# A windowed attention and channel mix on one core: unit 0's q and k loaded in halves of four heads, with all orders and choices found anew

## The chip, the core and the metric

One core of a Trainium2 chip runs the whole program. PE is the matrix engine, ACT, DVE and POOL are the scalar, vector and general engines, and SP issues the DMA transfers. The metric is the device time of one execution in microseconds; lower is better.

## The reference

Attention over 4 batches of 8 heads, 768 positions and head size 64, with a window of 128 positions and 4 sink positions that every query sees; its output is the input `x` of a channel mix with a shift by one position.

```python
scores = scale * np.matmul(q, k.transpose(0, 1, 3, 2))
keep = is_sink | ((rel >= 0) & (rel < window))        # rel = query position - key position
scores = np.where(keep, scores, -1e9)
a = softmax(scores);  attn = np.matmul(a, v)          # (4, 8, 768, 64)
x = attn.transpose(0, 2, 1, 3).reshape(4, 768, 512)
xk = mu_k * x + (1 - mu_k) * x_prev                   # x_prev: x, one position later
xr = mu_r * x + (1 - mu_r) * x_prev
k = np.maximum(xk @ w_k, 0.0)                         # 512 x 1024
v = k * k @ w_v                                       # 1024 x 512
out = 1 / (1 + np.exp(-(xr @ w_r))) * v
```

## The kernel before

The work is cut into 12 units `u` of 256 positions, three for each batch (T = 0, 1, 2). For each unit the kernel does four things.

`load` issues the transfers of q, k and v from SP's queue into fp32 buffers (`qs`, `ks`, `vs`, three each). For the early units a buffer holds eight heads as 1 KB pieces (four positions of one head), and two transfers of 64 partitions each bring one tensor: one for each value of `w`, and each brings pieces of all eight heads.

`prepare` casts a half (four heads) at a time to bf16 (`kb`, `qb`, on ACT, DVE or POOL), transposes it on PE into a bank, and copies the bank to `kt` or `qt` (ACT or DVE). Units from 4 (k) and 8 (q) on are transposed by DMA instead. `vb` is v in bf16, also cast by one of the three engines. A half's cast waits for both transfers of its tensor.

`attend` makes scores for two heads at a time into one of two tiles `sc`, in pairs (chunks 0 and 2, then 1 and 3; a chunk is two heads). ACT writes the exponentials (`e`), DVE multiplies them by a mask (`e<-e,mask`), or, in units 0 and 1, PE has added the mask's bias to `sc` beforehand. The sink positions have scores and exponentials of their own (`es`). PE multiplies by `vb`, DVE divides (`rec`, `x`).

`mix` transposes `x` to `xt` and forms `td`, `xk` and `xr` on DVE. `ffn` makes the products: eight blocks with w_k (`keys`, 32 matmuls of 256 columns), ReLU and square (`rl`, `kk`, on ACT or DVE), the gate with w_r (`gate`, and `th` on ACT), and the values with w_v (`product`), which DVE multiplies by the gate and SP stores. The weights come as fp32 (`w`) and are cast on chip in quarters (`wk_sb`, `wv_h`) or halves (`wr_sb`).

No scheduler orders this when the program is built. Each step is an operation with a number, in the order in which the code makes it. Three tables, found beforehand by a search with planned durations and written out as numbers, decide the rest: `ORDER` is the order in which operations are emitted, and so the order of each engine's queue and of SP's; a negative number there is a fill, a matmul on `warm` with no use. `CHOICE` gives an operation to another engine than its usual one. `SLOTS` says which buffer of a pool each tile takes. An engine takes its instructions strictly in that order, and waits at each for the semaphores that it needs.

Of the kernel before, what the change touches and what calls it, by code (L numbers as in the profile page):

```python
# [8 lines left out]
FP32 = mybir.dt.float32  # L9
# [9 lines left out]
    92: "ACT", 93: "ACT", 94: "ACT", 95: "ACT", 97: "ACT", 100: "ACT", 102: "DVE", 105: "DVE",  # L19
    110: "DVE", 111: "DVE", 114: "ACT", 115: "DVE", 139: "POOL", 142: "POOL", 145: "POOL", 148:  # L20
    "DVE", 150: "DVE", 151: "ACT", 152: "ACT", 154: "DVE", 161: "DVE", 191: "DVE", 193: "DVE",
    194: "DVE", 197: "DVE", 199: "DVE", 200: "DVE", 203: "DVE", 204: "DVE", 213: "DVE", 230:
    "ACT", 234: "ACT", 273: "DVE", 276: "DVE", 279: "DVE", 282: "DVE", 285: "ACT", 286: "ACT",
    298: "DVE", 306: "DVE", 315: "ACT", 354: "DVE", 364: "ACT", 365: "DVE", 367: "DVE", 383:
    "ACT", 387: "ACT", 436: "DVE", 439: "DVE", 444: "DVE", 445: "DVE", 467: "ACT", 475: "ACT",
    514: "DVE", 516: "DVE", 521: "DVE", 524: "ACT", 525: "ACT", 546: "ACT", 550: "ACT", 554:
    "ACT", 558: "ACT", 595: "DVE", 598: "DVE", 603: "ACT", 604: "ACT", 606: "DVE", 634: "ACT",
    681: "DVE", 682: "DVE", 691: "DVE", 700: "ACT", 704: "ACT", 708: "ACT", 755: "DVE", 759:
    "DVE", 760: "ACT", 772: "DVE", 781: "ACT", 785: "ACT", 789: "ACT", 834: "DVE", 836: "DVE",
    837: "DVE", 853: "ACT", 856: "DVE", 857: "ACT", 860: "DVE", 861: "ACT", 904: "DVE", 906:  # L30
    "DVE", 910: "DVE", 912: "DVE", 913: "DVE", 929: "ACT", 933: "ACT", 940: "DVE", 941: "ACT",
    994: "DVE", 995: "ACT", 999: "ACT", 1003: "ACT", 1007: "ACT", 1022: "DVE", 1026: "DVE",
    1034: "DVE", 1035: "ACT",
# [20 lines left out]

VS = ()
# [130 lines left out]
def kernel(  # L186
# [14 lines left out]
    nc = tc.nc  # L201
# [14 lines left out]
    P = Plan()  # L216
# [28 lines left out]
    buf = P.buf  # L245
# [829 lines left out]
```

## Time and profile before

| | |
|---|---|
| timed runs, median of 3 (lowest, highest) | 165.98 us (165.54 to 166.24) |
| profiled execution: span from first to last instruction | 164.3 us; the page gives no other time of it |
| PE busy, DVE, ACT, POOL | 158.4, 145.4, 131.2, 13.5 us |
| DMA | 34.6 MB, 79042 packets, 86.3% of 16 engines' span in SP's queue |
| fill matmuls (L1018) | 30 |

Busy times overlap. PE's matmuls are pipelined and their ends are modelled, so the spacing of their starts says more than their durations. A line of the timeline gives the start, the busy time, the engine, the line of the kernel, the operation, what is written and read, how many instructions are merged, and in brackets how long the engine sat idle before and what released it. SPq is SP's DMA queue; its time is that of issuing, not of moving bytes.

### The profile page before, as it was taken

To read this page: it belongs to the slowest core of one execution; us is meant where nothing else is said; L and a number is where in the kernel's file an instruction comes from. 1 tells how busy PE (TensorE), PEld (TensorE's weight loads), DVE (VectorE), ACT (ScalarE), POOL (GpSimd) and SP (SyncE) were. 2 spreads that over 40 slices of the span, in tenths; PEclk is the share of its full clock that TensorE was granted. 3 is DMA by queue.
4 is the path that set the end of the run, shared out by engine and by line. 5 is a ranking of instruction groups with operands and counts; after the bars stand their busy time and mean duration, and the time that the engine had idled before them with its cause. 6 is when DMAs were issued, how large, how long until landed. Compare 5 with 4: busy or idle time off the path is not lost.

```text
span 164.3 us, 4195 instructions
## 1 busy us (share of the span) xinstructions
PE 158.4 (96%) x1603; PEld 102.6 (62%) x1603; DVE 145.4 (89%) x381; ACT 131.2 (80%) x218; POOL 13.5 (8%) x38
## 2 busy tenths in 40 slices
PE   6999889999999999999999999999999999999992
PEld 2455568866467587577566775856575765664851
DVE  5259999999999999989999999999999999789752
ACT  3277999999999999999999999997668759163240
POOL 6409300010000000060000000000000000000000
PEclk9999999999999999999999999999999999999999
DMA  4999999999969896999999887986996955077743
GB/s 120 247 305 311 348 335 355 301 354 210 228 154 270 135 240 148 234 198 167 224 216 157 188 156 163 235 146 150 199 123 136 362 149 200 0 90 297 262 185 128
DMA packets 79042, 34.60 MB, mean 211 GB/s; under 512 B 67112, under 2 KB 73520, under 8 KB 79024
## 3 DMA queue, kind: packets, MB, share of 16 engines
q1 hardware_dynamic: 79008, 34.35, 86.3%
q8 instruction: 12, 0.20, 0.6%
q14 instruction: 6, 0.05, 0.1%
q10 hardware_dynamic: 16, 0.00, 0.0%
HBM read 24.12 MB, written 6.29 MB: 185 GB/s over the span
## 4 chain that ended last, share of the span: by engine, by line
PE 79%; ACT 8%; SPq 4%; DMA 3%; issue 2%; DVE 1%; POOL 1%; DVEq 0%; ACTq 0%; POOLq 0%
PE bank L997 23%; PE bank L939 23%; PE bank L979 12%; PE bank L808 6%; PE sc L721 6%; SPq L337 3%; DMA qs<-in_q_dram 3%; PE bank L576 2%; ACT e L775 2%; PE bank L849 2%; ACT rl L949 1%; PE bank L763 1%; ACT qt L589 1%; PE bank L909 1%; PE bank L1018 1%
## 5 line engine op out<-in xcount | busy, mean ns | idle before, releaser
L775 ACT ACTIVATE e<-sc 128x1024 bf16<-128x1024 f32 (+1 forms) x48 | 46.1, 994 | 1.8 <-PE sc L721 1.7
L939 PE MATMUL bank<-xk,wk_sb 128*128 128x256 bf16 x384 | 47.1, 273 | 0.0
L997 PE MATMUL bank<-wv_h,kk 128*128 128x512 bf16 x184 | 43.1, 379 | 0.1
L939 PEld LDWEIGHTS <-wk_sb 128*128 128x128 bf16 x384 | 36.4, 98 | 7.4 <-issue 0.4
L949 ACT ACTIVATE rl<-bank 128x512 bf16<-128x512 f32 x40 | 24.2, 625 | 8.6 <-PE bank L939 7.1
L997 PEld LDWEIGHTS <-kk 128*128 128x128 bf16 x184 | 17.1, 98 | 17.8 <-issue 0.4
L789 DVE TENSOR_TENSOR e<-e,mask 128x1024 bf16<-128x1024 bf16 (+1 forms) x40 | 25.4, 642 | 0.7 <-ACT e L775 0.5
L979 PE MATMUL bank<-wr_sb,xr 128*128 128x512 bf16 x96 | 23.7, 379 | 0.0
L888 DVE SCALAR_TENSOR_TENSOR xk<-td,mu_all,xt 128x256 bf16<-128x256 bf16 x48 | 22.4, 483 | 0.3
L888 DVE SCALAR_TENSOR_TENSOR xr<-td,mu_all,xt 128x256 bf16<-128x256 bf16 x48 | 22.1, 475 | 0.2
L967 ACT ACTIVATE kk<-rl 128x512 bf16<-128x512 bf16 x29 | 18.3, 664 | 4.2 <-DVE rl L953 4.0
L985 ACT ACTIVATE th<-bank 128x512 f32<-128x512 f32 x24 | 15.1, 646 | 5.7 <-PE bank L979 5.7
L825 DVE TENSOR_TENSOR x<-bank,rec 128x256 bf16<-128x256 f32 x48 | 19.2, 416 | 0.4
L808 PE MATMUL bank<-vb,e 128*128 128x65 bf16 x352 | 16.6, 194 | 0.0
L1006 DVE SCALAR_TENSOR_TENSOR w<-th,bank 128x512 f32<-128x512 f32 x19 | 13.0, 682 | 3.6 <-issue 1.8
L808 PEld LDWEIGHTS <-e 128*128 128x128 bf16 x352 | 13.6, 97 | 3.5
L979 PEld LDWEIGHTS <-xr 128*128 128x128 bf16 x96 | 8.8, 98 | 8.6 <-issue 0.2
L721 PE MATMUL sc<-qt,kt 64*128 64x128 bf16 (+1 forms) x256 | 13.9, 238 | 0.0
L721 PEld LDWEIGHTS <-kt 64*128 64x128 bf16 x256 | 8.9, 94 | 5.7 <-issue 3.1
L1018 PE MATMUL bank<-warm 128*128 128x512 bf16 x30 | 10.6, 484 | 1.1 <-DVE warm L1038 1.1
L877 DVE TENSOR_TENSOR td<-xt 128x512 bf16<-128x512 bf16 x24 | 10.3, 428 | 0.7 <-ACT xt L858 0.5
L589 ACT COPY qt<-bank 128x512 bf16<-128x512 bf16 x15 | 9.4, 643 | 1.0 <-PE bank L576 1.0
(74 smaller groups left out, 161.7 us busy)
## 6 DMA issues: line engine op xcount, KB each, us to landing
ks<-in_k_dram SPq DMA_DIRECT2D x24, 256.0 KB, 4.7
qs<-in_q_dram SPq DMA_DIRECT2D x24, 256.0 KB, 4.4
vs<-in_v_dram SPq DMA_DIRECT2D x24, 256.0 KB, 4.4
out_dram<-w SPq DMA_DIRECT2D x19, 256.0 KB, 2.7
w<-in_moe_w_k_dram SPq DMA_DIRECT2D x2, 1024.0 KB, 10.4
w<-in_moe_w_v_dram SPq DMA_DIRECT2D x2, 1024.0 KB, 9.3
w<-in_moe_w_r_dram SPq DMA_DIRECT2D x1, 1024.0 KB, 9.7
out_dram<-ob SPq DMA_DIRECT2D x4, 256.0 KB, 2.6
```

Source lines behind the costliest of these rows:

```text
L721: nc.tensor.matmul(out=sc[:, a, o0:o1], lhsT=lhs[rows], rhs=rhs[rows], start=u not in BIAS, stop=True, skip_group_check=u in BIAS)
L775: nc.scalar.activation(out=buf[ek][:, :, lo:], in_=buf[sck][:, :, lo:], func=AF.Exp, scale=scale)
L789: nc.vector.tensor_tensor(out=at, in0=at, in1=m, op=ALU.mult)
L808: nc.tensor.matmul(out=o[:, g, a, :], lhsT=e[:, a, e0:e0 + 128], rhs=rhs, start=(T == 0 and i == 0), stop=(i == len(blocks) - 1), skip_gro ...
L825: P.op("DVE", dve(256), lambda ok=ok, rk=rk, c=c: nc.vector.tensor_tensor(out=buf["x", u][:, :, 128 * c:128 * c + 128].rearrange("p g (a d ...
L888: nc.vector.scalar_tensor_tensor(out=buf[key][:, c, :], in0=buf[tk][:, i, :], scalar=mu[w][:, c:c + 1], in1=xt[:, c, t0 - 1:t0 + 255], op0 ...
L939: nc.tensor.matmul(out=ps[:, i, :], lhsT=wk_sb[:, c, 128 * f:128 * f + 128], rhs=xk[:, c, :], start=(c == 0), stop=(c == NC - 1), skip_gro ...
L949: nc.scalar.activation(out=buf[rk], in_=buf[psk].rearrange("p (i t) -> p i t", i=2), func=AF.Relu)
L967: nc.scalar.activation(out=buf["kk", u][:, 2 * f2:2 * f2 + 2, :], in_=buf[rk], func=AF.Square)
L979: nc.tensor.matmul(out=buf[psk], lhsT=buf["xr", u][:, c, 128 * g:128 * g + 128], rhs=wr_sb[:, c, :], start=(c == 0), stop=(c == NC - 1))
L985: P.op("ACT", act(512), lambda psk=psk, tk=tk: nc.scalar.activation(out=buf[tk], in_=buf[psk], func=AF.Tanh, scale=0.5), rank + 4 + g, tak ...
L997: nc.tensor.matmul(out=buf[psk], rhs=wv_h[:, f, :], lhsT=buf["kk", u][:, f, 128 * g:128 * g + 128], start=(f == 0), stop=(f == NF - 1))
```

## The change

Unit 0's q and k come head-wise. Each of the four transfers becomes two, of four heads each: 64 partitions with two pieces of 1 KB instead of four. Both transfers of the first half of q are issued first, then the two of k's first half. A half's cast waits only for its own two transfers. Further, 20 memsets of one column follow the mask on POOL. The steps and what they compute are the same otherwise. All three tables are new.

```diff
+BY_HALF = (0,)
...
 CHOICE = {
-    92: "ACT", 93: "ACT", 94: "ACT", 95: "ACT", 97: "ACT", 100: "ACT", 102: "DVE", 105: "DVE",
+    92: "DVE", 93: "ACT", 94: "ACT", 95: "DVE", 96: "DVE", 97: "DVE", 98: "DVE", 99: "ACT", 100:
...
 ORDER = (
-    80, 81, 78, 82, 87, 83, 84, 77, -1, -2, -3, -4, -1, -2, 90, 0, 1, 79, 102, 108, -2, -3, -4,
+    83, 81, 80, 78, 82, 2, 77, 0, 1, 3, 4, 5, 8, 9, 79, 105, -1, -2, -3, -4, -1, -2, -3, -4, 106,
...
+            if u in BY_HALF:
+                rows = src[b, :, 256 * T:256 * T + 256, :].rearrange(
+                    "(w l) (p j) d -> w p l (j d)", w=2, j=4)
+
+                def by_half(key=key, rows=rows, half=0):
+                    for w in range(2):
+                        nc.sync.dma_start(
+                            out=buf[key][w::2, 4 * half:4 * half + 4, :, :].rearrange(
+                                "p (l x) j d -> p l (x j d)", x=2),
+                            in_=rows[w][:, 2 * half:2 * half + 2])
+
+                for half in range(2):
+                    P.op("SP", 650.0, lambda f=by_half, half=half: f(half=half), rank,
+                         service=800.0, descs=256,
+                         take=[] if half else [(name + "s", key)], hold=[key] if half else [],
+                         writes=[(name, u, half, w) for w in range(2)])
+                continue
...
+    spare = tile1([128, 20], FP32, "spare")
+
+    def short(engine, lo, hi):
+        for i in range(lo, hi):
+            engine.memset(spare[:, i:i + 1], 0.0)
...
     def make_mask():
         window_mask(mask.rearrange("p k q -> p (k q)"), ones, 0.0)
+        short(nc.gpsimd, 0, 20)
```

In the listings below `x2` counts equal rows, and the number behind a name is that of the buffer. First SP's queue at the start of the program: ks_67 and qs_70 take unit 0, ks_68 and qs_71 unit 1, ks_69 and qs_72 unit 2. Before:

```order
L337 DMA ks_67<-in_k_dram 64x4x256 x2
L337 DMA qs_70<-in_q_dram 64x4x256 x2
L307 DMA vs_73<-in_v_dram 128x8x64 x2
L337 DMA ks_68<-in_k_dram 64x4x256
L337 DMA qs_71<-in_q_dram 64x4x256 x2
L337 DMA ks_68<-in_k_dram 64x4x256
L307 DMA vs_74<-in_v_dram 128x8x64
```

And in the change:

```order
L355 DMA qs_70<-in_q_dram 64x2x256 x2
L355 DMA ks_67<-in_k_dram 64x2x256 x4
L355 DMA qs_70<-in_q_dram 64x2x256 x2
L322 DMA vs_73<-in_v_dram 128x8x64 x2
L370 DMA qs_71<-in_q_dram 64x4x256 x2
L370 DMA ks_68<-in_k_dram 64x4x256 x2
```

Eight transfers stand ahead of v's instead of four, and unit 1's k is whole before anything of unit 1's v.

Next ACT's queue from unit 1's first exponentials (e_97) to the first cast of w_k (wk_sb) and what follows it; kt_86 and qt_90 are unit 1's, kt_87 and qt_91 unit 2's. Before:

```order
L775 ACTIVATE e_97<-sc_62 128x1024
L775 ACTIVATE e_93<-sc_61 128x1024
L589 COPY kt_86<-bank_63 128x2x256
L703 ACTIVATE es_98<-bank_66 128x256
L589 COPY qt_91<-bank_64 128x2x256
L646 CAST vb_136<-vs_74 128x8x64
L775 ACTIVATE e_94<-sc_61 128x1024
L589 COPY qt_91<-bank_65 128x2x256
L775 ACTIVATE e_95<-sc_62 128x1024
L703 ACTIVATE es_99<-bank_65 128x256
L501 ACTIVATE wk_sb<-w_76 128x4x256
L858 COPY xt_155<-bank_65 128x2x256
```

And in the change, from the copy behind the first two exponentials on:

```order
L629 COPY kt_86<-bank_65 128x2x256
L629 COPY qt_91<-bank_63 128x2x256
L629 COPY kt_87<-bank_66 128x2x256
L743 ACTIVATE es_98<-bank_64 128x256
L815 ACTIVATE e_93<-sc_62 128x1024
L815 ACTIVATE e_95<-sc_61 128x1024
L629 COPY kt_87<-bank_65 128x2x256
L815 ACTIVATE e_96<-sc_61 128x1024
L815 ACTIVATE e_94<-sc_62 128x1024
L629 COPY qt_91<-bank_63 128x2x256
L541 ACTIVATE wk_sb<-w_76 128x4x256
L743 ACTIVATE es_99<-bank_64 128x256
```

Unit 2's first two exponentials (e_96, e_94) and its copies now stand ahead of w_k's cast, and unit 1's v is no longer cast there.

Last DVE's queue up to the first products; td, xk_113 and xr_117 are unit 0's, x_108 unit 1's, xk_114 unit 1's. Before:

```order
L888 SCALAR_TENSOR_TENSOR xk_113<-td_111,mu_all,xt_155 128x256
L822 RECIPROCAL rec_101<-bank_66 128x4
L888 SCALAR_TENSOR_TENSOR xr_117<-td_111,mu_all,xt_155 128x256
L825 TENSOR_TENSOR x_108<-bank_66,rec_101 128x2x128
L822 RECIPROCAL rec_102<-bank_63 128x4
L825 TENSOR_TENSOR x_108<-bank_63,rec_102 128x2x128
L877 TENSOR_TENSOR td_112<-xt_155 128x512
```

And in the change:

```order
L865 TENSOR_TENSOR x_108<-bank_65,rec_102 128x2x128
L862 RECIPROCAL rec_101<-bank_64 128x4
L829 TENSOR_TENSOR e_96<-e_96,mask 128x1024
L865 TENSOR_TENSOR x_108<-bank_64,rec_101 128x2x128
L898 COPY xt_155<-bank_66 128x2x256
L547 CAST wk_sb<-w_76 128x4x256
L917 TENSOR_TENSOR td_112<-xt_155 128x512
```

DVE now casts a quarter of w_k itself (and another five rows further down), and multiplies an exponential of unit 2 by its mask ahead of that. On PE, all 24 score matmuls of unit 2 stand ahead of the first product with w_k, where none did before.

More of the change, by code (lines that the diff above doesn't have):

```diff
@@ L18 @@
 CHOICE = {
-    92: "ACT", 93: "ACT", 94: "ACT", 95: "ACT", 97: "ACT", 100: "ACT", 102: "DVE", 105: "DVE",
[L20 to L30, printed above, removed]
@@ L31 @@
-    "DVE", 910: "DVE", 912: "DVE", 913: "DVE", 929: "ACT", 933: "ACT", 940: "DVE", 941: "ACT",
-    994: "DVE", 995: "ACT", 999: "ACT", 1003: "ACT", 1007: "ACT", 1022: "DVE", 1026: "DVE",
-    1034: "DVE", 1035: "ACT",
+    92: "DVE", 93: "ACT", 94: "ACT", 95: "DVE", 96: "DVE", 97: "DVE", 98: "DVE", 99: "ACT", 100:
+    "ACT", 101: "DVE", 102: "POOL", 104: "DVE", 105: "ACT", 107: "DVE", 108: "DVE", 110: "DVE",
+    111: "POOL", 113: "ACT", 114: "DVE", 115: "DVE", 139: "DVE", 141: "ACT", 142: "POOL", 144:
@@ new lines @@
+    "DVE", 145: "POOL", 147: "ACT", 148: "POOL", 150: "ACT", 151: "POOL", 152: "DVE", 154: "ACT",
+    161: "DVE", 191: "DVE", 193: "ACT", 194: "DVE", 196: "ACT", 197: "DVE", 199: "ACT", 200:
+    "DVE", 202: "ACT", 203: "ACT", 204: "DVE", 206: "DVE", 213: "DVE", 221: "ACT", 222: "DVE",
+    225: "DVE", 226: "DVE", 229: "ACT", 230: "ACT", 233: "ACT", 234: "DVE", 273: "ACT", 275:
+    "ACT", 276: "DVE", 278: "ACT", 279: "DVE", 281: "ACT", 282: "ACT", 284: "ACT", 285: "DVE",
+    286: "ACT", 291: "DVE", 298: "ACT", 306: "ACT", 307: "DVE", 310: "ACT", 311: "DVE", 314:
@@ new lines @@
+    "ACT", 315: "ACT", 318: "ACT", 319: "DVE", 354: "ACT", 356: "ACT", 358: "ACT", 359: "ACT",
+    361: "ACT", 363: "ACT", 364: "ACT", 365: "DVE", 367: "DVE", 374: "ACT", 382: "ACT", 383:
+    "ACT", 386: "ACT", 387: "DVE", 390: "ACT", 391: "ACT", 394: "ACT", 395: "ACT", 434: "DVE",
+    436: "ACT", 438: "ACT", 439: "DVE", 441: "ACT", 443: "ACT", 444: "ACT", 445: "DVE", 447:
+    "DVE", 454: "DVE", 462: "ACT", 463: "DVE", 466: "ACT", 467: "DVE", 470: "ACT", 471: "DVE",
+    474: "ACT", 475: "DVE", 514: "ACT", 516: "ACT", 518: "ACT", 519: "DVE", 521: "ACT", 523:
@@ new lines @@
+    "ACT", 524: "DVE", 525: "ACT", 530: "ACT", 537: "DVE", 545: "ACT", 546: "ACT", 549: "ACT",
+    550: "ACT", 553: "ACT", 554: "ACT", 557: "ACT", 558: "ACT", 593: "ACT", 595: "DVE", 597:
+    "ACT", 598: "DVE", 600: "ACT", 602: "ACT", 603: "ACT", 604: "ACT", 606: "DVE", 613: "ACT",
+    621: "ACT", 622: "DVE", 625: "ACT", 626: "ACT", 629: "ACT", 630: "ACT", 633: "ACT", 634:
+    "ACT", 673: "DVE", 675: "ACT", 677: "ACT", 679: "ACT", 681: "DVE", 682: "ACT", 684: "ACT",
+    691: "ACT", 699: "ACT", 700: "DVE", 703: "ACT", 704: "ACT", 707: "ACT", 708: "ACT", 711:
@@ new lines @@
+    "ACT", 712: "ACT", 751: "DVE", 753: "ACT", 755: "DVE", 757: "ACT", 759: "DVE", 760: "ACT",
+    765: "DVE", 772: "ACT", 780: "ACT", 781: "ACT", 784: "ACT", 785: "ACT", 788: "ACT", 789:
+    "ACT", 792: "ACT", 793: "ACT", 828: "ACT", 830: "ACT", 832: "DVE", 834: "DVE", 836: "DVE",
+    837: "ACT", 852: "ACT", 853: "ACT", 856: "ACT", 857: "DVE", 860: "ACT", 861: "ACT", 864:
+    "ACT", 865: "ACT", 904: "DVE", 906: "ACT", 908: "ACT", 910: "DVE", 912: "DVE", 913: "ACT",
+    928: "DVE", 929: "ACT", 932: "ACT", 933: "ACT", 936: "DVE", 937: "DVE", 940: "ACT", 941:
@@ L34 @@
+    "ACT", 994: "ACT", 995: "DVE", 998: "ACT", 999: "ACT", 1002: "ACT", 1003: "DVE", 1006: "ACT",
+    1007: "ACT", 1022: "DVE", 1023: "ACT", 1026: "DVE", 1027: "ACT", 1030: "ACT", 1031: "ACT",
+    1034: "ACT", 1035: "DVE",
 }
```

156 rows, old and new, of tables (ORDER, SLOTS) are left out of this document.

## The prediction

> **What bounds the kernel now.** I read the page first, for the shares and the chain of waits that ended last.
>
> ```profile
> span 164.3 us, 4195 instructions
> PE 158.4 (96%) x1603; PEld 102.6 (62%) x1603; DVE 145.4 (89%) x381; ACT 131.2 (80%) x218; POOL 13.5 (8%) x38
> PE 79%; ACT 8%; SPq 4%; DMA 3%; issue 2%; DVE 1%; POOL 1%; DVEq 0%; ACTq 0%; POOLq 0%
> ```
>
> The span is that of the profiled execution; the timed runs' median, 165.98, lies 1.7 us above it, and I carry that 1.7 over. PE's 96% includes fill matmuls (L1018), so the next view is busy time by stretches, cut where the chain first reaches a product of the channel mix (L939) and where PE ends.
>
> ```profile
> core 0: us, PE busy (x) PEld busy (x) DVE busy (x) ACT busy (x) POOL busy (x), PEclk, DMA share, GB/s
> 24.13:60.00 35.87, 35.83 (x383) 24.54 (x383) 35.27 (x93) 35.56 (x59) 0.74 (x2) 1.00 0.98 253
> 60.00:73.00 13.00, 12.94 (x153) 9.48 (x150) 12.25 (x31) 12.94 (x24) 2.50 (x2) 1.00 0.89 192
> 73.00:161.05 88.05, 88.00 (x853) 56.80 (x852) 80.57 (x205) 66.25 (x113) 0.39 (x2) 1.00 0.82 180
> ```
>
> From 24.13 us to the end of its work PE is idle for 0.15 us of 136.9; since the ends of matmuls are modelled, some tenths may be hidden, and I allow 0.5 in all. ACT and DVE are full beside it until 73, but PE does not wait for them. So a new order can win almost nothing after 24 us; it can only lose there. What is left to win lies ahead of it: the first product should start early, with as much of PE's work as possible behind it. The timeline of that part:
>
> ```profile
> 0.81 1.41 SPq L337 DMA_DIRECT2D ks<-in_k_dram  x2
> 2.27 1.27 SPq L337 DMA_DIRECT2D qs<-in_q_dram  x2
> 3.58 1.23 SPq L307 DMA_DIRECT2D vs<-in_v_dram  x2
> 4.84 0.62 ACT L543 CAST kb<-ks 128x512 bf16<-128x512 f32 x1 [1.66 <-DMA ks<-in_k_dram]
> 7.61 0.43 DVE L543 CAST qb<-qs 128x512 bf16<-128x512 f32 x1 [2.31 <-DMA qs<-in_q_dram]
> 9.76 0.43 DVE L646 CAST vb<-vs 128x512 bf16<-128x512 f32 x1
> 9.91 1.51 ACT L775 ACTIVATE e<-sc 128x768 bf16<-128x768 f32 x2
> 12.64 0.86 POOL L543 CAST qb<-qs 128x512 bf16<-128x512 f32 x1 [6.67 <-DMA qs<-in_q_dram]
> 13.48 0.62 POOL L543 CAST kb<-ks 128x512 bf16<-128x512 f32 x1
> 16.68 1.94 ACT L775 ACTIVATE e<-sc 128x1024 bf16<-128x1024 f32 x2 [0.31 <-PE sc L721]
> ...
> 22.85 0.47 DVE L888 SCALAR_TENSOR_TENSOR xk<-td,mu_all,xt 128x256 bf16<-128x256 bf16 x1
> 22.85 1.08 ACT L501 ACTIVATE wk_sb<-w 128x1024 bf16<-128x1024 f32 x1
> 23.98 0.77 PEld L939 LDWEIGHTS <-wk_sb 128*128 128x128 bf16 x8 [0.34 <-ACT wk_sb L501]
> 27.59 1.06 ACT L775 ACTIVATE e<-sc 128x1024 bf16<-128x1024 f32 x1
> ```
>
> Unit 0's k is there at 4.84, its q at 7.61, its first exponentials run at 9.91. Unit 1's q lands at 12.6 and its k by 13.48, its exponentials start at 16.68. The first product starts at 23.98, when ACT has cast a quarter of w_k (22.85); unit 2's exponentials come after it, at 27.59.
>
> **The change, part by part.** *Unit 0's loads.* Four transfers become eight of half the size. An issue takes about 0.65 us whatever it moves (1.41, 1.27 and 1.23 above for two; the v pieces are 1024 of 256 B, the k pieces 256 of 1 KB). So the first four, one half of q and of k, are issued by 3.5, where k and q whole were issued in the same time. Today k lands 2.6 after its second issue ends (2.22); with half the bytes I take 2.0 to 2.5: q's half at 4.2, k's at 5.5. All eight are issued at 6.15 instead of 3.54, and the second halves land at 7 and 8.2. v's issues move from 3.58 to 6.2, past four issues more; today v waits behind q's bytes, so of these 2.6 us some 0.9 remain: v at 9.7 and 10.6. What follows in SP's queue (unit 1's q and k, then unit 2's, v, w_k) moves by the same 0 to 0.9; I take unit 1's q at 12.4 and its k at 13.9, between today's 13.48 and 0.9 later.
>
> *Unit 0's chain.* Durations for this and the following walk, from the timeline, the chain of waits, and the groups by shape:
>
> ```profile
> 8.77 0.59 ACT L589 COPY qt<-bank 128x512 bf16<-128x512 bf16 x1 [0.72 <-PE bank L576]
> 26.28 1.27 DVE L888 SCALAR_TENSOR_TENSOR xk<-td,mu_all,xt 128x256 bf16<-128x256 bf16 x3
> 18.99 0.75 DVE L543 CAST kb<-ks 128x512 bf16<-128x512 f32 x2
> 21.58 0.75 DVE L825 TENSOR_TENSOR x<-bank,rec 128x256 bf16<-128x256 f32 x2
> 32.81 0.55 PE sc L721 x12
> 35.87 0.22 PE bank L576 x4
> 37.82 0.22 PE bank L849 x4
> 65.14 0.93 ACT e L775
> 67.06 0.28 ACT es L703
> 68.75 0.48 ACT qt L589
> L501 ACT ACTIVATE wk_sb<-w 128x1024 bf16<-128x1024 f32 x4 | 4.2, 1092 | 0.0
> L505 DVE TENSOR_SCALAR wv_h<-w 128x1024 bf16<-128x1024 f32 x3 | 2.0, 677 | 0.0
> ```
>
> Back to back an instruction follows 0.08 to 0.1 after less than its duration: 0.40 for L888, 0.335 for casts and x, 0.6 for a copy from a bank. From a cast's end to the copy of its transposes are 0.73 (8.04 to 8.77). q's cast on ACT 4.3 to 4.95, DVE's copy 5.7 to 6.4; k's cast on POOL 5.5 to 6.2, DVE's copy 6.9 to 7.6; scores 7.7, exponentials 8.1: 1.8 earlier than today, and the second pair 10.9 against 12.80 in the same view.
>
> *Unit 1 does not inherit it.* DVE casts k of unit 1 when it has landed (14.0), PE transposes, ACT copies at 15.1, exponentials at 16.1: 0.6 earlier than today.
>
> *From there to the first product two queues decide.* On ACT stand, ahead of w_k's first cast, six exponentials (0.95), five copies (0.49), one es (0.29) and the cast itself (0.95): 9.4 from 16.1, so 25.5. Two of the six are unit 2's and wait for scores behind unit 1's values, whose v DVE casts only at 20.9; that costs 0.85: 26.35. On DVE, from 15.3 (cast, x and copy after unit 1's k) to the end of its w_k cast: eight L888 (3.2), two td and two xt (1.66), five casts (1.68), four rec (0.5), four x (1.34), one mask product (0.6), w_k (0.68), 9.65, so 25.0; it waits 0.1 for unit 2's k, 0.4 for PE and 0.6 for the exponential that the mask product needs (to 24.0): 26.1. The first product starts at 26.2, 2.2 later than at 23.98.
>
> *What PE has done by then.* All of unit 2's scores now stand ahead of it (24 matmuls more, 1.1), four transposes of q and k more (0.22) and four of x (0.22): 1.5. Net 0.7 lost. The fills, 28 for 30, only fill waits and cost nothing.
>
> *Behind the first product.* Sixteen matmuls of the first two blocks run 1.75 to 27.95; the third needs ACT's second w_k cast, behind one es and one exponential: 26.35 + 0.3 + 0.95 + 0.95 = 28.55. That is 0.6 of waiting. Bounds: 0, if the hidden tail covers it, and 1.0, if ACT is late by another 0.4. Today's 0.15 to 0.5 stand in the same place, so I set 0.35 against it.
>
> *Work between engines.* Counting both orders with these durations, DVE gives up some 2.2 us in sum, ACT takes 0.8, POOL three more casts (2.5 by the 0.86 row). After 24 us PE covers all of it; price 0. POOL also gets 20 short memsets ahead of its cast of unit 1's v. Their nearest rows:
>
> ```profile
> 0.34 0.11 POOL L1056 MEMSET const-float32-1.0<- 128x1 f32 x1
> 0.41 0.11 POOL L1056 MEMSET const-uint8-127<- 128x1 uint8 x1
> ```
>
> Two starts lie 0.035 apart, so 0.7 to 2.2 in all. POOL's casts, masks and memsets then end at 19.0 to 20.4 and the cast at 19.8 to 21.2, while PE needs DVE's half of the same v, at 20.9: hidden, at worst 0.3.
>
> *Sum.* 164.3 + 0.7 + 0.6 - 0.35 = 165.25, to which I add nothing for waits later on; with 1.7 that is **167.0**, 0.6% slower. About 0.5% is what a measurement of this kernel can tell from no change.
>
> **Fills and clock.** The fills start 0.43 apart up to 7 us and 0.22 apart after it:
>
> ```profile
> 4.17 3.03 PE L1018 MATMUL bank<-warm 128*128 128x512 bf16 x7
> 8.79 0.81 PE L1018 MATMUL bank<-warm 128*128 128x512 bf16 x3
> ```
>
> So PE ran at half speed for its first six microseconds, which the clock column (1.00 throughout) does not show. Today it is fed without a gap from 1.13 to 7; in the new order eight fills end at 4.6 and the transposes come at 5.0. If that gap makes PE stay slow to about 10 us, unit 0's biases, transposes and scores take twice as long, 0.9 on its chain. Of that 0 to 0.9 reaches the first product; by the walk above 0, since unit 1's loads end last. [...]
>
> **Rivals.** *The head start carries through (faster).* If half transfers keep the engines as full as whole ones, unit 1's k is in at 13.4 instead of 13.9, and if DVE and ACT also find no waits (1.1 and 0.85 above), the first product starts at 24.6 to 25.0 with the 1.5 done, and w_k's second cast is in time: 0.6 to 1.0 - 1.5 - 0.35, or 163.1 to 163.4; with 1.7, 164.7 to 165.1. It decides from a first product at 25.0 on down. For it speaks the 6.67 us that POOL sits idle for q; against it, that ACT's and DVE's queues hold 9.4 and 9.65 us of work between unit 1's start and the product, loads or not. *Loads late in the middle (slower still).* The weights w_r and w_v now stand behind unit 3's q and all of v. DMA share is 0.98 from 24 to 60 us, so a stream that is 0.9 late stays late, and the gate products and values wait for casts that wait for w_r. With 1 to 2 us of it: 168 to 169. Against it: nothing after 24 us waits for a load today. *Nothing moves:* the later product, the larger stock of exponentials and today's own hidden waits cancel: 165.7 to 166.8.
>
> **How the numbers follow.** Forecast (first product at 25.8 to 26.6, PE full after it), 166.5 to 167.6: 0.42. Nothing moves: 0.2. Head start carries: 0.22. Late loads: 0.16. The likeliest gives 167.0. The range reaches from the head start's 164.7 to 168.6, which leaves out some 0.1 at each end. Faster by over 0.5% (under 165.15): 0.21. Within: 0.2 + a third of the forecast = 0.33. Slower (over 166.8): 0.46.
>
> **What would show it.** Eight issues of about 0.6 us ahead of v; first exponentials at 8.1, unit 1's at 16.1; the first product (L979) at 26.2, released by w_k's cast or DVE; a wait of 0.6 before the third block; then PE without idle to the end. I am wrong if the first product starts before 25.0, if unit 1's k lands with today's or earlier, or if PE idles after 30 us by more than 0.5.

## The result, and the profile after

The changed kernel takes 168.64 us, median of 4 runs (168.28 to 169.3), against 166.02 for the kernel before on the same chip: a ratio of 1.0155, 95% interval 1.0126 to 1.0184. It is slower, by 2.6 us; the forecast was 167.0, the range's upper end 168.6. Here and below, medians leave out the few disturbed executions. The page of an execution that took 168.28:

```profile
span 166.6 us, 4216 instructions
PE 158.0 (95%) x1601; PEld 101.9 (61%) x1601; DVE 142.6 (86%) x375; ACT 132.0 (79%) x221; POOL 16.4 (10%) x61
PE 74%; DVE 7%; DMA 6%; ACT 6%; SPq 4%; issue 2%; DVEq 0%; ACTq 0%
```

PE's busy time is nearly what it was (158.4); the chain that ended last now goes through transfers for 6% of the span (before: 3%). Its start, from the timelines of SP's queue, ACT, DVE, POOL and PE:

```profile
0.80 1.41 SPq L355 DMA_DIRECT2D qs<-in_q_dram  x2
2.26 2.55 SPq L355 DMA_DIRECT2D ks<-in_k_dram  x4
4.86 1.25 SPq L355 DMA_DIRECT2D qs<-in_q_dram  x2
6.16 1.23 SPq L322 DMA_DIRECT2D vs<-in_v_dram  x2
...
4.15 0.62 ACT L583 CAST qb<-qs 128x512 bf16<-128x512 f32 x1 [0.98 <-DMA qs<-in_q_dram]
7.67 1.51 ACT L815 ACTIVATE e<-sc 128x768 bf16<-128x768 f32 x2 [2.90 <-PE sc L761]
16.77 1.94 ACT L815 ACTIVATE e<-sc 128x1024 bf16<-128x1024 f32 x2 [0.17 <-PE sc L761]
25.83 1.08 ACT L541 ACTIVATE wk_sb<-w 128x1024 bf16<-128x1024 f32 x1
...
11.22 0.43 DVE L686 CAST vb<-vs 128x512 bf16<-128x512 f32 x1 [0.63 <-DMA vs<-in_v_dram]
14.56 0.43 DVE L583 CAST kb<-ks 128x512 bf16<-128x512 f32 x1
...
14.61 0.84 POOL L583 CAST kb<-ks 128x512 bf16<-128x512 f32 x1 [0.28 <-DMA ks<-in_k_dram]
...
27.23 6.38 PE L979 MATMUL bank<-xk,wk_sb 128*128 128x256 bf16 x56
```

Unit 0's first exponentials run at 7.67 instead of 9.91. Nothing behind them inherits it: v's second cast at 11.22 (before: 9.76), unit 1's k cast at 14.61 (13.48), unit 1's exponentials at 16.77 (16.68), the first product at 27.23 (23.98).

PE's idle time does not show where the 2.3 us of span went, so I count differently. Each matmul is given the spacing of its back-to-back starts in the trace (0.109 us for a product with w_k, 0.216 for one of 512 columns, 0.055 for a transpose, 0.045 and 0.037 in attention; fills nothing). The two prices for attention are means over a group with its tail, the same that the prediction used for scores (0.55 for 12). That makes 147.2 us of work in both kernels, and elapsed time less work done is time lost up to that point:

| us lost up to | first product | 35 us | 75 | 98 | 120 | 160 |
|---|---|---|---|---|---|---|
| before | 12.82 | 13.00 | 13.93 | 13.88 | 13.86 | 13.64 |
| after | 14.54 | 14.74 | 14.98 | 14.52 | 16.25 | 15.81 |

Three parts, then. The start costs 1.7: the first product is 3.25 us later, with 12.69 - 11.16 = 1.53 more work done. From 35 to 98 us the new orders are better by 1.1, for before loses 0.9 there without an idle gap that the profile shows, and after loses nothing; what in the new orders wins it stays open. From 98 to 120 us after loses 1.7. The differences between the kernels hold better than the absolute values: with the spacing of starts alone in attention (0.028 or 0.055 for a score matmul of 128 or 256 columns, 0.031 for one with v), from 35 to 98 us before loses 3.0 and after 2.0, and the three parts come to 1.9, 1.0 and 1.8. That last stretch, by windows, first of before, then of after:

```profile
98.00:118.00 20.00, 20.00 (x213) 12.85 (x212) 19.59 (x54) 18.45 (x31) 0.00 (x0) 1.00 0.95 178
```

```profile
98.00:118.00 20.00, 18.84 (x193) 11.89 (x191) 17.39 (x48) 16.96 (x30) 0.51 (x2) 1.00 0.90 179
```

The profile shows PE idle there for 1.2 us, and for none in before. The chain there in after, in order of time (start, us, what):

```profile
95.62 0.58 SPq L332
96.20 0.04 issue
96.24 4.92 DMA vs<-in_v_dram
101.18 0.63 ACT vb L686
101.81 0.04 issue
101.86 0.52 PE bank L848 x12
```

Unit 8's second half of v is issued at 96.24, behind loads for units 9 to 11, lands after 4.9 us, and ACT casts it that moment. ACT's queue is in order, so what stands behind a cast that waits for a load waits too. The waits of ACT and of PE behind 60 us in after (engine, line, what it waited for: us in total, times, longest):

```profile
ACT qb L576 <- DMA qs<-in_q_dram: 0.9, 1, 0.9
ACT vb L686 <- DMA vs<-in_v_dram: 0.7, 1, 0.7
...
PE bank L979 <- ACT xt L898: 0.7, 1, 0.7
PE bank L848 <- ACT vb L686: 0.4, 1, 0.4
```

ACT's wait for that v ends at 101.18, the one for q at 111.49; they are 1.6 us together, and PE's two waits behind them 1.1. In before neither ACT nor DVE waits for a transfer anywhere behind 30 us, and PE has no wait in that list.

### The profile page after: what moved, and what is told of

Read it like the earlier page. It is cut to its first block, busy times and chain, and to the rows that moved or that the text cites. A ratio compares the mean times of both kernels' runs of the same rounds, so it can differ in the third digit from the quotient of the medians.

```text
span 166.6 us, 4216 instructions
## 1 busy us (share of the span) xinstructions
PE 158.0 (95%) x1601; PEld 101.9 (61%) x1601; DVE 142.6 (86%) x375; ACT 132.0 (79%) x221; POOL 16.4 (10%) x61
## 4 chain that ended last, share of the span: by engine, by line
PE 74%; DVE 7%; DMA 6%; ACT 6%; SPq 4%; issue 2%; DVEq 0%; ACTq 0%
PE bank L979 22%; PE bank L1037 21%; PE bank L1019 11%; PE bank L848 6%; DMA vs<-in_v_dram 6%; PE sc L761 5%; SPq L355 3%; PE bank L616 2%; PE bank L889 2%; DVE x L865 1%; PE bank L1058 1%; PE bank L803 1%; ACT rl L989 1%; ACT e L815 1%; PE bank L949 1%
## 5 line engine op out<-in xcount | busy, mean ns | idle before, releaser
L815 ACT ACTIVATE e<-sc 128x1024 bf16<-128x1024 f32 (+1 forms) x48 | 44.9, 973 | 5.5 <-PE sc L761 5.5
L1037 PE MATMUL bank<-wv_h,kk 128*128 128x512 bf16 x184 | 44.6, 379 | 0.0
L989 ACT ACTIVATE rl<-bank 128x512 bf16<-128x512 f32 x43 | 25.0, 606 | 8.9 <-PE bank L979 8.8
L928 DVE SCALAR_TENSOR_TENSOR xr<-td,mu_all,xt 128x256 bf16<-128x256 bf16 x48 | 22.7, 477 | 0.0
L928 DVE SCALAR_TENSOR_TENSOR xk<-td,mu_all,xt 128x256 bf16<-128x256 bf16 x48 | 21.9, 486 | 0.0
L1007 ACT ACTIVATE kk<-rl 128x512 bf16<-128x512 bf16 x30 | 19.0, 649 | 0.2 <-DVE rl L993 0.2
L848 PEld LDWEIGHTS <-e 128*128 128x128 bf16 x352 | 14.2, 97 | 5.9 <-issue 1.2
L761 PE MATMUL sc<-qt,kt 64*128 64x128 bf16 (+1 forms) x256 | 13.9, 238 | 0.3
L710 POOL COPY ksink<-kt 64x16 bf16<-64x16 bf16 x8 | 5.2, 653 | 78.6 <-PE bank L1019 31.9
L862 DVE RECIPROCAL rec<-bank 128x4 f32<-128x4 f32 x48 | 8.1, 176 | 5.2 <-PE bank L848 3.7
L1058 PE MATMUL bank<-warm 128*128 128x512 bf16 x28 | 8.9, 452 | 1.7 <-DVE warm L1078 1.1
```

Source lines behind the costliest of these rows:

```text
L761: nc.tensor.matmul(out=sc[:, a, o0:o1], lhsT=lhs[rows], rhs=rhs[rows], start=u not in BIAS, stop=True, skip_group_check=u in BIAS)
L815: nc.scalar.activation(out=buf[ek][:, :, lo:], in_=buf[sck][:, :, lo:], func=AF.Exp, scale=scale)
L848: nc.tensor.matmul(out=o[:, g, a, :], lhsT=e[:, a, e0:e0 + 128], rhs=rhs, start=(T == 0 and i == 0), stop=(i == len(blocks) - 1), skip_gro ...
L928: nc.vector.scalar_tensor_tensor(out=buf[key][:, c, :], in0=buf[tk][:, i, :], scalar=mu[w][:, c:c + 1], in1=xt[:, c, t0 - 1:t0 + 255], op0 ...
L989: nc.scalar.activation(out=buf[rk], in_=buf[psk].rearrange("p (i t) -> p i t", i=2), func=AF.Relu)
L1007: nc.scalar.activation(out=buf["kk", u][:, 2 * f2:2 * f2 + 2, :], in_=buf[rk], func=AF.Square)
```

## The experiments

All ratios are to the kernel before, run beside them on the same chip; it took 166.1 to 166.3 us each time.

**The load without the orders, the orders without the load.** Two kernels exchange one of the two parts. In the first, besides, the first scores and exponentials are moved ahead of the second halves' work, in the second only this differs:

```diff
-BY_HALF = (0,)
+BY_HALF = ()
```

> The orders and choices of before, with unit 0's q and k loaded head-wise alone (k first half, q first half, then the second halves; the first scores and exponentials moved ahead of the second halves' work). Theory: the four added issues of about 0.65 us put 2.6 us ahead of v and of unit 1's loads on SP's queue, so that the first exponentials come at about 8.3 us instead of 9.9, but v's casts at about 11 instead of 9.3 and 9.8, and unit 1's last k cast about 1.2 us later than its 13.5 to 15.0; unit 1's first exponentials at 17.3 to 17.9 instead of 16.7 and a time of 166.3 to 167.3 us against 166.0. Rival, that the orders alone cost the time and the head start is worth something by itself: unit 1's exponentials no later than 16.7 and 165.0 to 166.0 us.

> The orders and choices of after, with unit 0's q and k loaded in four whole pieces as before. Theory: half of the loss (some 1.5 of 2.4 us) sits at 95 to 115 us and belongs to the orders, so it stays; the start gains from v and unit 1's inputs being issued 2.6 us earlier and loses the early first scores: 167.2 to 168.3 us against 168.6 for after. Rival, that the new orders need the early first half: later first exponentials (about 9.5 instead of 7.7) push all that follows, 169 to 170 us. If the head-wise load were the whole cause, it would come to 166.0.

Old orders with the head-wise load: 168.09 us, ratio 1.0117 (1.0085 to 1.0148). New orders with whole loads: 171.91 us, 1.0362 (1.0321 to 1.0403). So the load, with the moves that go with it here, costs 2.0 us where I expected 0.3 to 1.3, and the rival that blamed the orders alone falls. The second run goes to its rival, by more than that had said: the new orders are fitted to the early half and lose 3.3 us more without it. In their issue order q's second transfer stands behind both of k's; unit 0's first exponentials run at 12.17 and the first product at 30.53. In the first kernel's trace (of its fastest execution, 167.63) the first product stands at 25.07, 1.1 later than before's, and the count of lost time stays 1.1 above before's from there to the end.

Of the 2.0 us, 1.4 lie in the span (median 165.7 against 164.3). The rest lies outside it: the time exceeds the span by 2.3 us here and by 1.8 in before. In this trace a load of instructions moves behind the span's end (165.3 us), ending 2.6 us after it:

```profile
q14 instruction: 1, 0.01, 0.3%
```

The same stands in the traces of the four other kernels below that have the old orders throughout and eight issues, and their times exceed the spans by about as much. In before, in after and in all other traces nothing moves there, and the difference is 1.7 to 2.1. Whether that load causes the 0.5 us stays open; what these five kernels cost by their work is what their spans show.

**Number of issues, or size of pieces.** Before's four issues of 256 KB were cut into eight of 128 KB, with nothing else changed; then four of the eight, those of q, went to ACT's queue, where they are issued ahead of ACT's first cast (operations 2 and 3 move up in `ORDER`, right behind 79).

```diff
+                for half in range(2) if u == 0 else (slice(None),):
+                    ls = slice(2 * half, 2 * half + 2) if u == 0 else half
-                        out=buf[key][w::2].rearrange("p (l x) j d -> p l (x j d)", x=2),
-                        in_=rows[w]
+                        out=buf[key][w::2].rearrange("p (l x) j d -> p l (x j d)", x=2)[:, ls],
+                        in_=rows[w][:, ls])
...
+                    queue = nc.scalar if key == ("q", 0) else nc.sync   # second kernel only
```

> Before, with each of unit 0's four issues of q and k (256 KB) cut into two of 128 KB, one right behind the other; bytes, orders, choices and what the casts wait for stay. Theory (at the start the issues set the pace: 128 KB in 0.65 us is 200 GB/s, where before moved 365 to 383 GB/s between 3.0 and 4.0 us): less than 5.0 MB moved in the first 20 us against 5.25, unit 0's last q cast and v's casts some 1.0 to 1.5 us later, the first product at 25 us instead of 24.0, 167.0 to 168.2 us. Rival, that the head-wise kernel with the old orders lost its 2.0 us to the casts and scores moved with it, or to the pattern of the transfers: 165.8 to 166.6 us here.

> Before with unit 0's eight pieces of 128 KB, the four of q issued by ScalarE's queue (from about 3.2 us, behind its table load) instead of SP's; ScalarE's cast of k's second half moves from 4.84 to about 5.6 us, which the wait for q covers. Theory (the number of issues on SP's queue set the pace, so that v and unit 1 came 2.6 us late): v is issued at 3.6 us as in before, 5.0 MB or more in the first 20 us, 166.0 to 166.9 us. Rival (the small pieces themselves move slowly, whoever issues them): the first 20 us move 4.7 to 4.8 MB as with eight issues on one queue, 167.5 to 168.4 us.

Eight issues on SP's queue: 168.04 us, 1.0105 (1.0077 to 1.0134), first product at 25.79. With q's four on ACT's queue: 166.54 us, 1.0029 (1.0008 to 1.0051), first product at 23.97. The pieces are the same in both, so 1.5 of the 1.9 us are the place that four more issues take in SP's queue. No cost of the pieces shows: with two queues the span is 164.2 (median) against before's 164.3, and the 0.4 left is the part outside the span. Windows of before (share and GB/s are the last two columns):

```profile
3.00:4.00 1.00, 0.88 (x4) 0.04 (x1) 0.42 (x7) 0.18 (x1) 0.93 (x4) 1.00 1.07 374
3.00:8.00 5.00, 4.88 (x20) 1.92 (x18) 1.25 (x9) 1.34 (x3) 2.90 (x11) 1.00 0.96 275
6.00:8.00 2.00, 2.00 (x13) 1.00 (x12) 0.39 (x1) 0.54 (x1) 0.00 (x0) 1.00 1.12 282
```

of after:

```profile
3.00:4.00 1.00, 1.00 (x4) 0.30 (x2) 0.41 (x1) 0.17 (x1) 0.87 (x5) 1.00 0.60 178
3.00:8.00 5.00, 4.75 (x33) 2.08 (x31) 2.17 (x4) 1.11 (x3) 3.42 (x10) 1.00 0.67 197
6.00:8.00 2.00, 1.86 (x22) 0.97 (x21) 1.23 (x3) 0.33 (x1) 1.76 (x5) 1.00 0.69 198
```

of before with eight issues:

```profile
3.00:4.00 1.00, 1.00 (x4) 0.18 (x1) 0.42 (x7) 0.18 (x1) 0.93 (x4) 1.00 0.60 179
3.00:8.00 5.00, 4.23 (x22) 1.67 (x20) 1.27 (x9) 1.28 (x3) 2.95 (x11) 1.00 0.67 192
6.00:8.00 2.00, 1.23 (x9) 0.48 (x7) 0.43 (x1) 0.94 (x2) 0.02 (x1) 1.00 0.73 208
```

and with q's four on ACT's queue:

```profile
3.00:8.00 5.00, 4.92 (x21) 1.81 (x18) 1.01 (x9) 0.60 (x2) 2.95 (x11) 1.00 0.94 245
4.00:6.00 2.00, 2.00 (x6) 0.73 (x6) 0.43 (x1) 0.00 (x0) 2.00 (x8) 1.00 0.90 244
6.00:8.00 2.00, 1.92 (x13) 0.91 (x11) 0.16 (x1) 0.40 (x1) 0.02 (x1) 1.00 1.12 285
```

128 KB in an issue of 0.65 us is 202 GB/s, and that is what moves while one queue issues such pieces: 178 to 208 GB/s at a DMA share of 0.6 to 0.73. The transfer engines are idle for a third of the time from 3 to 8 us, in which the kernel needs them most. Before, with 256 KB in an issue, has them at a share of 1.07 from 3 to 4 us and of 0.96 to 8 us, though from 4 to 6 us it too falls to 0.73 to 0.76, which no run here explains. The Trainium skill ("DMA: Bandwidth & Descriptors", Issuing engines are not separate DMA queues) says that transfers run on the same 16 engines whoever issues them, so that issuing from several engines saves issue time alone, which it calls usually small. Here that saving is the 1.5 us: where issuing is the limit, it raises what is moved from 192 to 245 GB/s.

**The same remedy in the head-wise kernels.** Four tries took issues off SP's queue there. In after: q's second half by ACT, or k's first half. With the old orders: all of q by ACT, once with the loads of the mixing coefficients behind q's first half, once with them first and with the second halves' casts on DVE. Where a half's issues or casts had to come earlier for this, their operations moved up in `ORDER` as well.

```diff
+                        queue = nc.scalar if half and key[0] == "q" else nc.sync      # q_half_on_act_queue
+                        queue = nc.sync if half or key[0] == "q" else nc.scalar       # k_first_half_on_act
+                        queue = nc.scalar if key[0] == "q" else nc.sync               # the two with the old orders
-                        nc.sync.dma_start(
+                        queue.dma_start(
```

> After, with the two issues of q's second half of unit 0 given by ScalarE's queue instead of SP's, so that v and all behind it are issued 1.3 us earlier; ScalarE's first cast moves from 4.15 to about 4.4 us. Theory (issues are the limit at the start): v's casts at about 9.0 and 10.0 instead of 10.2 and 11.2, unit 1's last k cast at about 13.6 instead of 14.6, the first product at 26.3 to 26.8 instead of 27.3, 167.6 to 168.3 us. Rival (the transfers themselves are the limit, whoever issues them): the same landings within 0.4 us and 168.4 to 169.0 us.

> After, with the two issues of k's first half of unit 0 given by ScalarE's queue ahead of its other work, so that both first halves are issued by 2.2 us and all behind them on SP's queue 1.3 us earlier; ScalarE's first cast moves from 4.15 to about 5 us. Theory: the second halves, v and unit 1's k (14.6 us) come about 0.6 to 1.2 us earlier, some of the 1.7 us at the start comes back and the late loss of 1.3 to 1.5 us stays: 167.6 to 168.4 us. Rival (with q's second half on that queue it came out at 169.6 us, so two queues only share the transfer time): 168.4 to 169.8 us.

> Old orders with the head-wise load, q's four issues by ScalarE's queue (the first half at 0.8 us, the second behind the table load at about 4.3 us), k's four and then v by SP's. Theory: with v and unit 1's loads back at before's issue times the head start of the first scores is all that is left of the change: first exponentials at 7.5 to 8.7 us, unit 1's at 16.7 or before, 165.0 to 166.3 us, against 168.1 with all on SP's queue. Rival (pieces or shared transfer time): 167.3 to 168.3 us.

> Old orders with the head-wise load: the two loads of the mixing coefficients stay first on ScalarE's queue (in the two-queue run before they stood behind q, and TensorE waited 1.8 us for them at the start), then q's first half, the table load, q's second half; k's halves and then v on SP's queue as in before; VectorE casts k's and q's second halves, and all four exponentials of unit 0 stand ahead of v's first cast where they can. Theory: v at 9.3 to 10.3 us and unit 1's k at 13.4 are before's, the first exponentials at 7.5 to 8.7 us are early, and unit 1's come at 16.7 all the same, since they wait for its k: 165.6 to 166.7 us, so a head start in unit 0 is worth nothing. Rival, that the head start carries through: 164.4 to 165.4 us. Rival, that head-wise pieces cost in themselves: over 167 us.

> The kernel of the run with the old orders, the head-wise load and q on ScalarE's queue once more, for a trace of its start. Its five undisturbed times of 167.1 to 168.1 us have to come from one of these. Theory: the first exponentials come near 8 us, but the second halves share the transfers with v, so that v's casts come past 10.3 us and unit 1's exponentials past 17.0 us. Rival: v and unit 1 are on time (16.7 us) and the time goes behind 20 us to work that the moved casts and exponentials push back on ScalarE and VectorE. 167.1 to 168.2 us by both.

None gained. q's second half by ACT: 169.59 us, 1.0221 (1.018 to 1.0261); it went out beside k's first half, whose cast on POOL moved from 5.45 to 6.95 with its issue where it was, and the first exponentials from 7.67 to 9.85. k's first half by ACT: 168.67 us, 1.018 (1.0141 to 1.0219), no faster than after, though 4.94 MB instead of 4.67 moved in the first 20 us and POOL cast unit 1's k at 13.40 instead of 14.61; the first product moved from 27.23 to 26.96 only. In the new orders the landing of k is therefore not the only thing that holds the start: unit 0's first exponentials ran at 8.68 instead of 7.67, and DVE, whose work on unit 0 stands ahead, cast the other half of unit 1's k at 14.42 instead of 14.56. Old orders, first try: 169.96 us, spoiled by my own move, as PE's wait shows:

```profile
PE bank L504 <- DMA ob<-in_moe_mu_k_dram: 1.8, 1, 1.8
```

Second try: 167.7 us, 1.0083 (1.006 to 1.0106), and again 167.91, 1.0125 (1.0061 to 1.0188), 0.9 and 1.1 of it over before's in the spans. The trace of the repetition:

```profile
8.83 1.51 ACT L792 ACTIVATE e<-sc 128x768 bf16<-128x768 f32 x2 [0.43 <-PE sc L738]
11.46 0.62 ACT L663 CAST vb<-vs 128x512 bf16<-128x512 f32 x1
14.00 1.51 ACT L792 ACTIVATE e<-sc 128x768 bf16<-128x768 f32 x2 [1.91 <-PE sc L738]
17.65 1.94 ACT L792 ACTIVATE e<-sc 128x1024 bf16<-128x1024 f32 x2 [0.31 <-PE sc L738]
```

Unit 0's first exponentials are 1.1 earlier than before's, its second pair 1.2 later and unit 1's 1.0 later, while unit 1's k was cast at 13.74 (before: 13.48). Those are the signs that the last theory named (v's casts past 10.3, at 10.40 on DVE and 11.46 on ACT; unit 1 past 17.0), but not for its reason: neither cast of v waited for a transfer. They stood behind other work in DVE's and ACT's queues. So work is displaced, ahead of 20 us and not behind it as the rival had it, and the displaced order was mine. Whether a head start in unit 0 is worth anything with an order found for punctual loads stays open; no run with the head-wise load came under before.

**The late loss.** First, after once more, unchanged, and after with one issue moved (operation 58, unit 8's second half of v, set right behind 57, its first half):

```diff
 ORDER = (
-    565, 591, 57, 68, 60,
+    565, 591, 57, 58, 68, 60,
...
-    71, 655, 58, 637, 568,
+    71, 655, 637, 568,
```

> After, unchanged, run beside the next three. Theory: the start (first exponentials near 7.7 us, the landing of unit 1's k at 14.6 us, the first product at 27.3 us) and the loss between 98 and 118 us belong to the program and come back in a second trace within 0.7 us each; 168.3 to 169.3 us. Rival, that they are chance of single transfers: the landing of unit 1's k and the late stretch differ by more than 1 us, in a time that stays at 168 to 170 us.

> After, with one issue moved: the second half of unit 8's v follows its first half (85.5 us) on SP's queue instead of standing behind loads of units 9, 10 and 11 (96.2 us). Theory: TensorE's wait of 0.41 us at 101.5 and ScalarE's of 0.72 us for that cast go, and of the 1.5 us lost between 98 and 118 us 0.5 to 1.2 come back: 167.4 to 168.1 us. Rival, that the stretch is lost to ScalarE's and VectorE's own queues and this wait is only where it shows: 168.3 to 168.9 us, with the wait found on another operand within a few us.

After again took 168.83 us, 1.0147 (1.0112 to 1.0182). The time lost by its first product, at 35 and at 75 us agrees with the first trace to 0.04. Behind that it differs: 15.72 lost at 98 us and 16.04 at 120 (first trace 14.52 and 16.25). The waits of ACT and PE behind 60 us:

```profile
ACT qb L576 <- DMA qs<-in_q_dram: 1.3, 1, 1.3
ACT vb L686 <- DMA vs<-in_v_dram: 0.4, 1, 0.4
...
PE bank L979 <- ACT xt L898: 1.0, 1, 1.0
```

So the start belongs to the program, as expected. The late loss comes back in about its size (1.3 us from 75 to 120 us in the first trace, 1.1 in the second) and not in its place: most of it here is unit 8's q, which ACT waits for until 76.69 us, ahead of an eviction of xt. The moved issue gave 169.58 us, 1.0223 (1.018 to 1.0266): no faster than after, and 0.9 slower by the medians. ACT no longer waits for that v, and in the traced execution (171.14, 1.6 above the median) it waits 2.7 us for q instead, 2.1 of them ahead of the place that was edited. The expectation fell.

Then the two q casts that had been late were moved behind the evictions of xt that they had held up (675 and 906), without and with an earlier issue of unit 8's v (58):

```diff
-    553, 597, 675, 503, 582,
+    553, 597, 503, 582,
-    588, 548, 679,
+    588, 548, 675, 679,
-    809, 722, 906, 823, 818,
+    809, 722, 823, 818,
-    771, 772, 781, 810,
+    771, 772, 906, 781, 810,
...
-    663, 542, 63, 65,          # second kernel only
+    663, 542, 58, 63, 65,
```

> After, with two casts of loaded q moved on ScalarE's queue: that of unit 8's first half (at 75.3 us) behind the next eviction of xt and the exponential after it, that of unit 11's first half (111.5 us) behind the next two exponentials and the next eviction of xt. Theory (the loads of the new orders land at the moment of their casts; a late one holds ScalarE, and with it the xt that TensorE's next product needs): TensorE's waits of 0.7 to 1.0 us for xt behind 70 us go, 167.2 to 168.1 us against 168.6 to 168.8. Rival, that the late half is short of ScalarE or VectorE time whatever stands first: the wait comes back on another operand, 168.3 to 169.2 us.

> The run before this one, and unit 8's second half of v issued ahead of four loads for units 9 to 11 instead of behind them (about 92 us instead of 96.2). Theory: ScalarE's wait of 0.4 to 0.7 us for that v goes as well, 166.8 to 167.8 us, which is after without its late loss (after minus 1.2 to 1.7). Rival, that each load moved ahead makes another one late: no faster than the run before it, 167.8 to 169 us.

169.53 us, 1.0198 (1.0166 to 1.023), and 168.53, 1.0148 (1.0117 to 1.0178). The waits in the first, ACT and PE:

```profile
ACT vb L686 <- DMA vs<-in_v_dram: 2.1, 1, 2.1
PE bank L848 <- ACT vb L686: 1.7, 1, 1.7
```

and in the second, DVE and PE:

```profile
DVE td L917 <- DMA xt<-x: 1.3, 1, 1.3
PE bank L979 <- DVE x L865: 1.1, 1, 1.1
```

The first edit freed the q casts, and unit 8's v came late by 2.1; the second freed that, and at 122 to 125 us a later v (0.4) and a transfer of x to xt (1.3) came late in its place. The second run is as fast as after, no faster. The late loss is no single misplaced issue; between 75 and 130 us the new orders ask for several loads at about the moment at which they land. It is theirs in every trace: in all eight of after and its variants, the one with whole loads among them, ACT waits for a load behind 60 us, and in none of those of before and its variants does ACT or DVE wait for a transfer behind 30 us.

**Which of the two owns the late loss.** Spliced kernels answer it: one kernel's loads, orders and choices up to a place where both have emitted nearly the same operations (about 42 to 44 us), the other's behind it, each with its own buffers. In words:

```diff
-ORDER = (all of before, or all of after)
+ORDER = (the first 292 places of before) + (what is left, in after's order)     # old_start_own_slots
+ORDER = (the first 296 places of after) + (what is left, in before's order)     # new_start_own_slots
```

> Before's loads, orders, choices and buffers for its first 292 places (to about 42 us), then after's, with after's own choice of buffers kept (the three spliced kernels that came out at 175 us had their PSUM banks dealt out anew). Theory, that the start holds the greater part of the loss and the rest of after can stand behind before's start: 165.6 to 167.2 us. Rival, that after's later orders fit only behind their own start, whatever the buffers: over 169 us.

> After's head-wise loads, orders, choices and buffers for its first 296 places (to about 44 us), then before's with its own buffers. Theory: the start's 1.7 to 2.1 us are lost and neither the late loss nor the middle's gain of the new orders follows: 167.4 to 168.5 us, with no wait for a load on ScalarE behind 60 us. Rival, that the late waits for loads follow from the start (a later unit 1, later buffers): ScalarE waits for a load behind 60 us and the time is 168.6 us or more.

Old start, new rest: 167.8 us, 1.0087 (1.0056 to 1.0118), slower than before by 1.7 with whole loads and before's start. That lies between the theory's range and the rival's, and how much of it is lost at the seam is not shown, for no trace near that time was kept. New start, old rest: 169.66 us, 1.0204 (1.0175 to 1.0233). Its total misses the expectation, since PE lost 1.4 us at the seam, from 40 to 45 us. Behind the seam it does as the theory says: 17.13 us lost up to 75, 17.33 up to 120, 17.11 up to 160, and neither ACT nor DVE waits for a transfer behind 30 us. So the late waits do not follow from the late start. That the new orders lose time behind either start is shown by the times; that they do so by the same waits behind before's start is not.

Three earlier splices, cut at place 220 or 218 (the third also at 700, about 98 us), had been given PSUM banks and some other buffers anew, by a rule of oldest release:

> Before's loads, orders and choices for its first 220 places (to about 33 us), then after's orders and choices for all that is left. Theory (the head-wise start costs 1.7 us, after's middle from 35 to 98 us is 1.0 us better than before's, its stretch from 98 to 118 us 1.5 us worse): 166.0 + 0.5 = 166.2 to 167.0 us. Rival one, everything is lost at the start: 164.8 to 165.5 us. Rival two, after's later orders hold only behind their own start: over 167.5 us.

> After's head-wise loads, orders and choices for its first 218 places (to about 33 us), then before's orders and choices. Theory: 1.7 us lost at the start and nothing given back: 167.4 to 168.4 us. Rival, the start is not where it is lost: 165.7 to 166.6 us.

> Before's first 220 places (to about 33 us), after's orders and choices from there to its place 700 (about 98 us), then before's. Theory: the start and the end of before with the middle of after, which loses 0.2 us of TensorE time between 35 and 98 us backwards (a gain) where before's loses 0.8: 164.8 to 165.6 us, faster than both. Rival, an order is worth what it is only behind its own past, so that the seams at 33 and 98 us cost what the middle gives: 165.8 to 167.5 us.

They came out at 175.67, 174.58 and 175.87 us, ratios 1.057, 1.0514 and 1.0575. The two that begin with before's orders lose most of it within 10 us of a seam; the third loses about 2 of its 6 us over after there and the rest later. Against the splices above, both the place of the cut (33 us there, 42 to 44 here) and the buffers differ, so the 5 to 8 us between them can't be put down to the one or the other; for the question of the late loss they say nothing.

## Why the prediction was wrong, step by step

- **Direction, and the first product's price:** right. The later first product buys more work: predicted 1.5 us of it, counted 1.53. The two agree because the count of matmuls (24 scores and eight transposes more) was read from the order rightly; the price of a score is the same in both, and with the spacing of starts it is 1.35.
- **Start of the first product, predicted 26.2, measured 27.23: the first step that failed.** The walk from unit 1's exponentials to the product holds roughly (10.1 us predicted, 10.46 measured; the sum took 26.2, though ACT's walk, the later of the two, had given 26.35). Its beginning was 0.67 late: unit 1's exponentials at 16.77 instead of 16.1, behind k casts at 14.56 (DVE) and 14.61 (POOL) instead of 13.9 to 14.0. That came from "of these 2.6 us some 0.9 remain" for v and all behind it in SP's queue; v was 1.5 later than before at its second cast and unit 1's k 1.1. I had counted the eight issues of 0.65 us correctly but had not asked what the transfer engines move while they are issued: it is 197 GB/s from 3 to 8 us, where before moves 275. The term that was too small is the 0.9. Net of the 1.53, the start cost 1.7 where the sum had 0.7.
- **The wait of 0.6 before the third block, less today's 0.35:** absent; 56 products run from 27.23 without a gap. ACT's second cast of w_k ended at 28.99, just as the first 16 products did, because the first product was late. From the first product to 35 us before loses 0.18 and after 0.20, so the 0.35 stands in neither.
- **"Today's 0.15 to 0.5" hidden behind 24 us, so that nothing can be won there:** wrong. By the count of work before loses 0.9 us from 35 to 98 us, and the new orders lose none of it. The idle time that the profile shows hid more than I allowed.
- **"I add nothing for waits later on": the step that failed most.** The 1.7 us from 98 to 120 stand where ACT waits for loads, 0.7 and 0.9 us; that these waits make up the whole of it is argued from place and size, since no edit won it back. I had the rival, loads late in the middle, at 0.16 with 168 to 169 us, where the time fell; but I looked for it in w_r and w_v, which were in time, and argued that nothing waits for a load today. That speaks of the old orders. What could have been read in the orders is the distance from an issue to its cast in each queue: unit 8's second half of v stands behind loads of units 9 to 11.
- **Fills and clock, memsets:** the 20 memsets took 0.88 us and hid; the fills cost nothing, and unit 0's exponentials came 0.4 earlier than predicted, so the 0 to 0.9 of the clock did not appear: four transposes took 0.61 us at 4.83 and 0.40 at 6.11, so PE had its full pace by then, in before by 7.04.

In sum: predicted 0.7 + 0.6 - 0.35 = 0.95 over before's span; measured 1.7 - 1.1 + 1.7 - 0.2 (won behind 120 us) = 2.2, in spans 2.3. That the total misses by only 1.3 is luck: a gain of 1.1 that the prediction held to be impossible stands against a loss of 1.7 that it put at nothing.

## What to carry to other kernels

When transfers are cut into smaller ones, compute bytes per issue over the time of an issue and hold it against what the engines move: with 128 KB in 0.65 us, 202 GB/s, the first half came earlier here and all that followed came later. Before a new order is trusted, list for every load how long before its cast it is issued, and compare that with the landing times of the trace; a cast in an in-order queue turns a late load into a wait of whatever stands behind it. Curing one such wait by hand moved it to the next load three times, so the slack has to come from the order as a whole.

## What was not expected of the hardware

An issue's pace, not the number or size of the pieces, set the bandwidth from 3 to 8 us: 192 GB/s with eight pieces of 128 KB on one queue, 245 with the same pieces on two. In five kernels a load of instructions behind the last instruction goes with 0.5 us more outside the span. Two executions of the same program agreed to 0.04 us in lost time up to 75 us; behind it the one waited 1.3 us for a q until 76.7, the other not at all there but 0.9 us for a q until 111.5. The transfers' times differ between executions. No trace of before or its variants shows such a wait behind 30 us, so the old orders leave enough time for it.
